# Turned x laid out by quarter, and the last batch's seven second-layer products in another order

## The chip, the cores and the metric

The kernel runs on one core of a Trainium2 chip. The metric is device time in microseconds (us) of one execution. Engines are named as the profile does: PE is TensorE's matmuls and PEld its weight loads, DVE is VectorE, ACT ScalarE, POOL GpSimd and SP the engine whose queue issues every DMA of this kernel. A name with a q behind it (SPq) is that engine's instruction queue.

## The reference

An attention with a local window and block sums, and behind it a mixer with two token layers and two channel layers:

```python
# q, k, v: (4, 8, 768, 64); block 32, window 16
k_sum, v_sum = k.reshape(B, H, 24, 32, D).max(3), v.reshape(B, H, 24, 32, D).mean(3)
scores_l = where(|i - j| < 16, scale * q @ k.T, -1e9)
scores_s = scale * q @ k_sum.T + log(32)
a = softmax(concat[scores_l, scores_s])            # with + 1e-9 in the sum
x = (a @ concat[v, v_sum]) -> (4, 768, 512)        # heads side by side
h  = relu(x.T @ w_tok1) @ w_tok2                   # 768 -> 256 -> 768 tokens
u  = x + h.T
h2 = relu(u @ w_ch1) @ w_ch2                       # 512 -> 1536 -> 512 channels
out = u + h2                                       # (4, 768, 512)
```

All in float32. The host lays inputs out and turns the result back; the kernel writes out as (batch, channel, token).

## The kernel before, in words

**Split operands.** A float32 product is made of three matmuls in the faster fp32r type: each operand is rounded (ACT, the "high" part), the rest is the difference (DVE or POOL, the "low" part), and high x high, high x low and low x high are summed in PSUM. The function `halved` makes such a pair.

**Stages.** Batches 0 to 2 go through attention, then token layers (`tok1*`, `tok2`), then the channel layers in 24 steps (two halves of tokens, twelve blocks of the 1536 channels): `ch1` (tile hp, result h) and `ch2` (tile acc). While batch b is in its channel layers, the attention of batch b + 1 runs between its steps. The last batch (b = 3) computes its channel layers in `last_batch` with seven products in place of eight (Winograd's form of Strassen's scheme): sums and differences of the four quarters of the weights ("mixed weights") and of u or h. POOL and ACT compute the mixed weights while batches 0 to 2 run (`mixes`, tiles wa and wc, which are stored to DRAM as mix_w1h, mix_w1l, mix_w2h, mix_w2l). `mixed_weight` loads one set back over a place in w1 or w2 that the products no longer need. Each set has a number, 0 to 3.

**Turning x.** For batches 2 and 3 (FAR = 2) the attention's result x, with tokens in the partitions, is turned so that channels are: DVE transposes each block of 32 x 32 (`turn_x`, L679, into tile xb), SP stores the tile to DRAM (L690, xaway), and SP fetches it in four parts of 32 partitions each (`fetch`, L571). In partition p of the DRAM tile stand the blocks of quarter q = p / 32, and part r of the fetch takes from each of the four quarters the blocks of r. Batch 2's land in tiles xT, batch 3's in the tiles uf (`sums_at`). `turn_blocks` turns the attention's weights e in the same way (tiles away and eT).

**Use of turned x.** In batch 2, `tok2` adds the token layers' result to xT (L922) and makes its two halves (L929 on ACT, L935 on DVE or POOL). In batch 3, `tok2_last` adds to uf (L1208), and `halved` makes the halves z (L1178, L1183); `turned` makes the differences of u (L1222).

**The last seven products.** They are named by their operand of h: "11", "21", "22", "4", "2", "3", "1" (before). Each is 36 matmuls in PSUM tiles pz, pz, pr, pv, pw, px, py (`sum_of`, L1232, two row blocks o = 0 and 1). `differ` makes differences of h (L1458), `operands` their halves (L1440, L1445 or `halved`); the halves stand in places that earlier weights or operands have left (`homes`). `into` and `summed` add a result to uf (L1256, L1509), `store` writes a finished row block (L1494).

**What sets the order.** Every instruction is given to a planner with an engine, a time that it is taken for, a rank, and what it reads and writes. The planner plays the run through with these times and writes each engine's instructions in the order that it finds; each engine then works through its queue in that order and waits in place. An issue on SP is played with 0.06 or 0.4 us on its queue, and a transfer with kb / 250 us of a common line and 2.2 us of landing. Slots of one tag are used in turn, with as many buffers as the tag has.

Of the kernel before, what the change touches and what calls it, by code (L numbers as in the profile page):

```python
# [199 lines left out]
def tile_attention_mixer(  # L200
# [343 lines left out]
    def turn_blocks(p, g):  # L544

        e = e_t[p, g]
        away = plan.slot(dram, [P, 2 * HS], F32, "away", f"away_{p}_{g}", 3)
        t_sb = sbuf([P, 2, HS], "e", f"eT_{p}_{g}", 3)
        for j in range(2):
            eT_t[2 * p + j, g] = (lambda j=j: t_sb.t[:, j]), [(t_sb, r) for r in range(P // 32)]  # L550
        add(
            "dve", 1.05, lambda: nc.vector.transpose(flat(e.t), flat(e.t)),
            reads=[(e, "ends")], writes=[(e, part) for part in PARTS], rank=R_ATT,
        )
        add(
            "sp", 0.4, lambda: nc.sync.dma_start(out=away.t, in_=flat(e.t)),
            reads=[(e, part) for part in PARTS], writes=[(away, 0)], kb=393,
        )

        state["turned"] = fetch(away, t_sb, lambda: flat(t_sb.t), 150)  # L560

    def flat(t):
        return t.rearrange("p j c -> p (j c)")

    def fetch(away, slot, view, kb, behind=()):


        def part(r):
            rows = slice(32 * r, 32 * (r + 1))
            src = away.t.rearrange("(q p) (t k) -> p t q k", p=32, k=P)  # L570
            nc.sync.dma_start(  # L571
                out=view()[rows].rearrange("p (t q c) -> p t q c", q=P // 32, c=32),
                in_=src[..., rows],
            )

        return [
            add(
                "sp", 0.4, lambda r=r: part(r), reads=[(away, 0)], writes=[(slot, r)], kb=kb,
                behind=behind,
            )  # L580
            for r in range(P // 32)
        ]
# [90 lines left out]
    def turn_x(b, p):  # L673

        x2, a = x_t[b, p]
        e = sbuf([P, S], "e", f"xb_{b}_{p}", 3)
        add(
            "dve", 1.05,
            lambda: nc.vector.transpose(  # L679
                e.t.rearrange("p (t c) -> p t c", c=P), x2.t[:, :, a, :]  # L680
            ),
            reads=x_keys(b, p), writes=[(e, 0)], rank=R_ATT,
        )
        for half, nt in enumerate(HT[b]):
# [4 lines left out]
            add(  # L689
                "sp", 0.4, lambda away=away, cs=cs: nc.sync.dma_start(out=away.t, in_=e.t[:, cs]),  # L690
                reads=[(e, 0)], writes=[(away, 0)], kb=nt // 2,
            )

    def fetch_x(b, half, p):
        if b == B - 1:
            slot = sums_at(half, p)
            return fetch(
                xa_t.pop((b, half, p)), slot, lambda: slot.t, HT[b][half] // 5, state["turned"]
            )
        tag, bufs = (("e", 3), ("ot", 2))[half]  # L700
        slot = xT_t[b, half, p] = sbuf([P, HT[b][half]], tag, f"xT_{b}_{half}_{p}", bufs)
        fetch(xa_t.pop((b, half, p)), slot, lambda: slot.t, HT[b][half] // 5)

    def spent(nt, quarter, half):

# [176 lines left out]
    def tok2(b, half, p):  # L882
# [34 lines left out]
        if far:  # L917
            xT = xT_t.pop((b, half, p))
            parts = [(xT, r) for r in range(P // 32)]
            add(  # L920
                "dve", spent(nt, 0.42, 0.6),
                lambda: nc.vector.tensor_tensor(  # L922
                    out=xT.t, in0=pt.t[:, :nt], in1=xT.t, op=ALU.add
                ),
                reads=[(pt, 0)], writes=parts, rank=R_EVAC,
            )
            add(
                "act", spent(nt, 0.38, 0.5),
                lambda: nc.scalar.activation(u.t[:, 0], xT.t, AF.Copy),  # L929
                reads=parts, writes=[(u, 0)], rank=R_EVAC,  # L930
            )
            eng, took = (("dve", spent(nt, 0.42, 0.62)), ("pool", spent(nt, 0.7, 1.2)))[half]
            add(
                eng, took,
                lambda: (nc.vector, nc.gpsimd)[half].tensor_tensor(  # L935
                    out=u.t[:, 1], in0=xT.t, in1=u.t[:, 0].bitcast(F32), op=ALU.subtract
                ),
                reads=[*parts, (u, 0)], writes=[(u, 1)], rank=R_EVAC,
            )
            return  # L940
# [248 lines left out]
    def tok2_last(half, p):  # L1189
        b, t1, u = B - 1, t1_t[B - 1, p], sums_at(half, p)  # L1190
        pt = bank(f"up_{b}_{half}_{p}", EIGHT if half else BANKS[1])

        def products():
            for k in range(DTOK // P):
                ks = slice(k * P, (k + 1) * P)
                for i, (w, part) in enumerate(((wt2h, 0), (wt2l, 0), (wt2h, 1))):
                    nc.tensor.matmul(  # L1197
                        pt.t[:, :HS], lhsT=t1.t[:, part, ks],
                        rhs=w.t[:, k, HS * half : HS * (half + 1)],
                        start=(k == 0 and i == 0), stop=(k == DTOK // P - 1 and i == 2),  # L1200
                    )

        add(
            "pe", 1.08, products, reads=t1_keys(b, p) + T2_KEYS, writes=[(pt, 0)], rank=R_ATT
        )
        add(
            "dve", 0.56,
            lambda: nc.vector.tensor_tensor(out=u.t, in0=pt.t[:, :HS], in1=u.t, op=ALU.add),  # L1208
            reads=[(pt, 0)], writes=rows4(u), rank=R_H,
        )  # L1210
# [51 lines left out]
    def last_batch():  # L1262
# [204 lines left out]
        for i in range(0, HF, 2):  # L1467
            differ(i, "11", "12", "11")
            differ(i, "12", "22", "12")
            differ(i, "22", "22", "11")  # L1470
            differ(i, "21", "21", "22")
        for n, of in (("4", "21"), ("2", "22"), ("3", "12"), ("1", "11")):
            operands(n, of, R_ATT)

        def sum_of(name, f0, c0, pts, begin, sets):
# [12 lines left out]
        def pair(name):  # L1488
            return [bank8(f"{name}{o}") for o in range(2)]

        def store(half, row, slot):
            add(
                "sp", 0.06,
                lambda: nc.sync.dma_start(  # L1494
                    out=out[b, row * P : (row + 1) * P, half * HS : (half + 1) * HS], in_=slot.t
                ),
                reads=rows4(slot), kb=196,
            )

        def us(half, row):  # L1500
            slot = sum_t[half, row]
            return slot, rows4(slot)

        def summed(half, row, x):

            slot, keys = us(half, row)
            add(
                "dve", 0.56,
                lambda: nc.vector.tensor_tensor(out=slot.t, in0=slot.t, in1=x.t, op=ALU.add),  # L1509
                reads=[(x, 0)], writes=keys, rank=R_EVAC,  # L1510
            )

        def into(pts, half, row, done=False):
            for o in range(2):
                out_of(pts[o], us(half, row + o), us(half, row + o))
                if done:
                    store(half, row + o, sum_t[half, row + o])
# [12 lines left out]
        into(v, 0, 2)  # L1530
        w = pair("pw")
        sum_of("2", 0, 0, w, True, None)
        for o in range(2):
            out_of(w[o], one(t[o]), one(t[o]))
            summed(1, o, t[o])
        x = pair("px")
        sum_of("3", HF, 0, x, True, None)
        for o in range(2):
            out_of(x[o], one(u3[o]), one(t[o]))
            summed(0, 2 + o, u3[o])  # L1540
            store(0, 2 + o, sum_t[0, 2 + o])
            summed(1, 2 + o, u3[o])
# [322 lines left out]
```

## Time and profile before

| | |
|---|---|
| Times of three runs | 567.02, 563.09, 565.91 us (median 565.91) |
| The profiled execution | 563.82 us, its span 562.0 us |
| PE busy | 547.2 us of the span |
| DVE, ACT, POOL busy | 333.0, 252.7, 246.6 us |
| Granted clock of TensorE, mean | 0.994 |
| DMA | 101.10 MB in 143279 packets |

The span is from the first to the last instruction of the profiled execution; the time is around it. In a row of instructions stand line, engine, operation, tile written, tiles read, shape, count, and in brackets how long the engine had stood idle before it and what it waited for. Rows that end in "x4" are several alike, told together. In rows of one source line the three numbers are the least, the median and the most of one instruction in ns.

### The profile page before, as it was taken

The page shows a single profiled execution, that of the slowest core. Times are in us where ns is not written, and L with a number is a line of the kernel's source. Part 1 is how long each engine was busy: PE and PEld are TensorE (multiplying, and loading weights), DVE is VectorE, ACT ScalarE, POOL GpSimd, SP SyncE. Part 2 cuts the span into 40 slices and gives each one's busy share as a digit, 9 for nine tenths or more (in the row PEclk, how much of TensorE's full clock was granted, in tenths as well). Part 3 has the DMA queues.
Part 4 walks back from the last instruction along what each step waited for, and adds up shares of the span by engine and source line. Part 5 has one row for each costly group of instructions (what it writes and reads, how often), then busy time and mean ns, then how long its engine had stood idle before and what let it go on. Part 6 is the DMA issues. An engine that isn't in the chain of part 4 may idle for free. (4 is left out here: it accounts for less than half of the span.)

```text
span 562.0 us, 12604 instructions
## 1 busy us (share of the span) xinstructions
PE 547.2 (97%) x4557; PEld 481.7 (86%) x4557; DVE 333.0 (59%) x922; ACT 252.7 (45%) x784; POOL 246.6 (44%) x362
## 2 busy tenths in 40 slices
PE   7889999999999999999999999999999998999997
PEld 4678888888999978888799987788889998999996
DVE  3788999979365355553553256344442047669973
ACT  4777675625585444322414334244333334356600
POOL 0316697834574932310068303468869753000000
PEclk9899999999999999999999999999999999999999
DMA  8953768755567147877685416888686545932732
GB/s 278 335 176 98 222 194 262 228 177 184 189 198 252 41 145 214 212 199 209 168 233 127 107 29 194 173 225 225 157 258 136 120 134 160 320 111 74 228 119 84
DMA packets 143279, 101.10 MB, mean 180 GB/s; under 512 B 88560, under 2 KB 123504, under 8 KB 143216
## 3 DMA queue, kind: packets, MB, share of 16 engines
q1 hardware_dynamic: 143216, 100.29, 61.7%
q8 instruction: 36, 0.59, 0.5%
q14 instruction: 27, 0.22, 0.1%
HBM read 70.18 MB, written 28.31 MB: 175 GB/s over the span
## 5 line engine op out<-in xcount | busy, mean ns | idle before, releaser
L1008 PE MATMUL acc<-h,w2h 128*128 128x256 f32 (+1 forms) x576 | 153.8, 339 | 0.0
L965 PE MATMUL hp<-u,w1h 128*128 128x256 f32 (+1 forms) x576 | 143.8, 339 | 0.0
L1008 PEld LDWEIGHTS acc<-h,w2h 128*128 128x128 f32 x576 | 100.6, 188 | 13.7 <-ACT h L977 1.6
L965 PEld LDWEIGHTS hp<-u,w1h 128*128 128x128 f32 x576 | 98.0, 189 | 12.4 <-issue 1.1
L491 ACT ACTIVATE e<-e,den 128x120 f32<-128x120 f32 x192 | 73.4, 384 | 52.5 <-DVE den L481 45.5
L965 PE MATMUL hp<-u,w1l 128*128 128x256 f32 (+1 forms) x288 | 96.9, 336 | 0.0
L1008 PE MATMUL acc<-h,w2l 128*128 128x256 f32 (+1 forms) x288 | 96.4, 335 | 0.0
L982 DVE SCALAR_TENSOR_TENSOR h<-hp,h 128x512 fp32r<-128x512 f32 (+1 forms) x72 | 39.9, 554 | 84.0 <-ACT h L977 83.8
L977 ACT ACTIVATE h<-hp 128x512 fp32r<-128x512 f32 (+1 forms) x72 | 35.1, 488 | 112.0 <-PE hp L965 111.2
L965 PEld LDWEIGHTS hp<-u,w1l 128*128 128x128 f32 x288 | 54.4, 189 | 5.8
L1008 PEld LDWEIGHTS acc<-h,w2l 128*128 128x128 f32 x288 | 54.2, 188 | 5.2
L481 DVE CUSTOM_DVE_ANT_0 e<-sc,mask_sb 128x120 f32<-128x120 f32 x192 | 41.7, 277 | 18.3 <-PE sc L467 16.8
L607 POOL TENSOR_SCALAR rec<-den 128x6 f32<-128x6 f32 x32 | 8.7, 272 | 66.9 <-ACT e L491 64.8
L491 ACT ACTIVATION_READ_ACCUMULATOR e<-e,den 128x1 f32 x192 | 36.1, 188 | 0.0
L1048 POOL TENSOR_TENSOR ot<-ot,u 128x512 f32<-128x512 f32 (+1 forms) x24 | 24.4, 1045 | 17.0 <-DVE ot L1040 15.4
L467 PE MATMUL sc<-k,q 64*64 64x120 f32 x768 | 29.5, 280 | 2.2 <-DVE den L481 2.0
L467 PEld LDWEIGHTS sc<-k,q 64*64 64x64 f32 x768 | 21.6, 138 | 11.2 <-issue 6.2
L906 PE MATMUL up<-wt2h,t 128*128 128x512 f32 (+1 forms) x96 | 28.4, 354 | 0.6 <-DVE t L725 0.6
L601 PEld LDWEIGHTS av<-v,eT 120*64 120x64 f32 x768 | 24.0, 138 | 4.9 <-issue 2.4
L601 PE MATMUL av<-v,eT 120*64 120x64 f32 x768 | 26.5, 224 | 1.0 <-DMA eT<-away 0.5
L335 DVE TENSOR_REDUCE ks<-k 128x24 f32<-128x768 f32 x16 | 15.2, 950 | 20.1 <-DMA k<-in_kw 20.1
L423 DVE TENSOR_REDUCE vs<-vb 96x8 f32<-96x256 f32 (+1 forms) x40 | 17.8, 459 | 13.0 <-DMA vb<-in_vb 12.8
(246 smaller groups left out, 1046.8 us busy)
## 6 DMA issues: line engine op xcount, KB each, us to landing
w<-in_w_ch SPq DMA_DIRECT2D x48, 256.0 KB
k<-in_kw SPq DMA_DIRECT2D x16, 720.0 KB
v<-in_vw SPq DMA_DIRECT2D x32, 288.0 KB
q<-in_q SPq DMA_DIRECT2D x16, 384.0 KB
away<-e SPq DMA_DIRECT2D x16, 384.0 KB
eT<-away SPq DMA_DIRECT2D x64, 96.0 KB
w<-in_w_tok SPq DMA_DIRECT2D x12, 256.0 KB
vb<-in_vb SPq DMA_DIRECT2D x32, 96.0 KB
```

The costliest lines, as they stand in the source:

```text
L335: lambda: nc.vector.tensor_reduce(out=ks.t.rearrange("p (t r) -> p t r", r=2), in_=kt.t[:, :, 16 : 16 + QT].rearrange("p t (r c) -> p t r ...
L423: lambda: nc.vector.tensor_reduce(out=s.t[:VB, rows], in_=slot.t[:VB], axis=AX, op=ALU.add),
L467: nc.tensor.matmul(tiles[j].t[c * QT : (c + 1) * QT, i * NC : (i + 1) * NC], lhsT=qt.t[rows, t * QT : (t + 1) * QT], rhs=kt.t[rows, t, :], ...
L481: nc.vector.tensor_tensor_reduce(out=e.t[:, j, i * P : i * P + NC], in0=tiles[j].t[:, i * NC : (i + 1) * NC], in1=mask_sb[:, mv, :], op0=A ...
L491: nc.scalar.activation(ei, ei, AF.Exp, bias=den_t[n].t[:, 1, T : T + 1], scale=-1.0, accum_out=den_t[n].t[:, 0, T : T + 1],)
L601: nc.tensor.matmul(pv[cs, T], lhsT=eT[:NC, T % (TT // 2), cs], rhs=v.t[:NC, 2 * T + c], start=True, stop=True,)
L906: nc.tensor.matmul(pt.t[:, :nt], lhsT=t1.t[:, part, ks], rhs=w.t[:, k, h0 : h0 + nt], start=(far and k == 0 and i == 0), stop=(k == DTOK / ...
L965: nc.tensor.matmul(pt.t[:, :nt], lhsT=block(w, f, c), rhs=us[c].t[:, part], start=(i == 0), stop=(i == len(ops) - 1),)
L977: lambda: nc.scalar.activation(h.t[:, 0], pt.t[:, :nt], AF.Relu),
L982: lambda: nc.vector.scalar_tensor_tensor(out=h.t[:, 1], in0=pt.t[:, :nt], scalar=0.0, in1=h.t[:, 0].bitcast(F32), op0=ALU.max, op1=ALU.sub ...
L1008: nc.tensor.matmul(slot.t[:, c0 : c0 + nt], lhsT=block(w, f, o), rhs=h.t[:, part], start=(f == 0 and w == "w2h" and part == 0 and o % n == 0),
L1048: lambda view=view, u=u: nc.gpsimd.tensor_tensor(out=view(), in0=view(), in1=u.t[:, 1].bitcast(F32), op=ALU.add),
```

## The change

Four things are changed.

1. `turn_x` writes its 32 x 32 blocks in the order (r, t, s) instead of (t, r, s): all blocks that part r will fetch stand side by side, for all six groups t of 128 tokens. One DMA stores the tile (before: one for each half of the tokens). `fetch_x` takes, from each of the four quarters q, one run: 384 bytes in batch 3, 512 and 256 bytes in batch 2 (before: runs of 128 bytes). The fetched tile's columns then stand in the order (q, t, s), quarter first.
2. What reads or adds to such a tile does so through permuted views (`from_sources`, `turned_to`, `turned_back`, `in_order`): in batch 2 the add and the two halves, after which u stands in the old order; in batch 3 the add of the token layers' result. The last batch's u stays in the new order through both channel layers, and the last add of each row block puts it back into the old order, into a tile of its own (tag t1), which is stored.
3. The last seven products run as "11", "21", "22", "2", "3", "1", "4". A21's differences and operand "4" come last. "3" is summed over the columns from c0 = 2 and "1" from c0 = 0, and three sets of mixed weights are loaded to other places: behind "11" set 2 (as before), behind "21" set 1, behind "22" set 0; none behind "4".
4. The planner is told of other sizes: 48 instead of 77 for a fetch of 48 KB, and one store of 393 instead of two.

```diff
-        state["turned"] = fetch(away, t_sb, lambda: flat(t_sb.t), 150)
+        state["turned"] = fetch(
+            away, t_sb,
+            lambda rows: away.t.rearrange("(q p) (t k) -> p t q k", p=32, k=P)[..., rows],
+            lambda t: flat(t).rearrange("p (t q c) -> p t q c", q=P // 32, c=32), 150,
+        )
...
-                e.t.rearrange("p (t c) -> p t c", c=P), x2.t[:, :, a, :]
+                e.t.rearrange("p (r t s) -> p t r s", r=P // 32, s=32),
+                x2.t[:, :, a, :].rearrange("p t (r s) -> p t r s", s=32),
...
-        for half, nt in enumerate(HT[b]):
-            cs = slice(H0[b][half], H0[b][half] + nt)
-            away = xa_t[b, half, p] = plan.slot(
-                dram, [P, nt], F32, f"xaway{nt}", f"xaway_{b}_{half}_{p}", 8
-            )
-            add(
-                "sp", 0.4, lambda away=away, cs=cs: nc.sync.dma_start(out=away.t, in_=e.t[:, cs]),
-                reads=[(e, 0)], writes=[(away, 0)], kb=nt // 2,
-            )
+        away = xa_t[b, p] = plan.slot(dram, [P, S], F32, "xaway", f"xaway_{b}_{p}", 8)
+        add(
+            "sp", 0.4, lambda: nc.sync.dma_start(out=away.t, in_=e.t),
+            reads=[(e, 0)], writes=[(away, 0)], kb=393,
+        )
...
+        fetch(
+            away, slot,
+            lambda rows: away.t.rearrange("(q p) (r t s) -> p r q t s", p=32, r=P // 32, s=32)[
+                :, rows.start // 32, :, ts
+            ],
+            from_sources, nt // 8, behind,
+        )
...
-                    out=xT.t, in0=pt.t[:, :nt], in1=xT.t, op=ALU.add
+                    out=from_sources(xT.t), in0=turned_back(pt.t[:, :nt]),
+                    in1=from_sources(xT.t), op=ALU.add,
...
-                lambda: nc.scalar.activation(u.t[:, 0], xT.t, AF.Copy),
+                lambda: nc.scalar.activation(in_order(u.t[:, 0]), turned_to(xT.t), AF.Copy),
...
-            lambda: nc.vector.tensor_tensor(out=u.t, in0=pt.t[:, :HS], in1=u.t, op=ALU.add),
+            lambda: nc.vector.tensor_tensor(
+                out=from_sources(u.t), in0=turned_back(pt.t[:, :HS]), in1=from_sources(u.t),
+                op=ALU.add,
+            ),
...
-            ("11", G0[:3]), ("21", [G0[3], *G1[:2]]), ("22", [*G1[2:], "x"]), ("4", ["v", "q", "x"]),
-            ("2", G0[:3]), ("3", [G0[3], *G1[:2]]), ("1", [*G1[2:], "x"]),
+            ("11", G0[:3]), ("21", [G0[3], *G1[:2]]), ("22", [*G1[2:], "x"]), ("2", ["v", "q", "x"]),
+            ("3", G0[:3]), ("1", [G0[3], *G1[:2]]), ("4", [*G1[2:], "x"]),
...
+            to = sbuf([P, HS], "t1", f"out_{half}_{row}", 4)
+            add(
+                "dve", 0.56,
+                lambda: nc.vector.tensor_tensor(
+                    out=turned_back(to.t), in0=from_sources(x()), in1=from_sources(slot.t),
+                    op=ALU.add,
+                ),
+                reads=[got, *keys], writes=[(to, 0)], rank=R_H,
+            )
...
-        sum_of("21", HF, 0, z, False, (0, HF, 0))
+        sum_of("21", HF, 0, z, False, (1, HF, 0))
...
-        sum_of("22", 0, 2, r, True, None)
+        sum_of("22", 0, 2, r, True, (0, 0, 1))
         into(r, 1, 0)
-        v = pair("pv")
-        sum_of("4", HF, 2, v, True, (1, HF, 1))
-        into(v, 0, 2)
...
-        sum_of("3", HF, 0, x, True, None)
+        sum_of("3", 0, 2, x, True, None)
...
-        sum_of("1", HF, 2, y, True, None)
+        sum_of("1", HF, 0, y, True, None)
         into(y, 1, 0, True)
         into(y, 1, 2, True)
+        v = pair("pv")
+        sum_of("4", HF, 2, v, True, None)
+        into(v, 0, 2, True)
```

More of the change, by code (lines that the diff above doesn't have):

```diff
@@ L558, in turn_blocks, with fetch @@
         )
-        state["turned"] = fetch(away, t_sb, lambda: flat(t_sb.t), 150)
+        state["turned"] = fetch(
[3 more added lines that the diff above has]
+        )
     def flat(t):
         return t.rearrange("p j c -> p (j c)")
[L565 to L573, printed above, removed]
-            )
+    def fetch(away, slot, src, view, kb, behind=()):
         return [
             add(
-                "sp", 0.4, lambda r=r: part(r), reads=[(away, 0)], writes=[(slot, r)], kb=kb,
-                behind=behind,
+                "sp", 0.4,
+                lambda r=r: nc.sync.dma_start(
+                    out=view(slot.t[32 * r : 32 * (r + 1)]), in_=src(slice(32 * r, 32 * (r + 1)))
+                ),
+                reads=[(away, 0)], writes=[(slot, r)], kb=kb, behind=behind,
             )
@@ L683, in turn_x, with from_sources, turned_to, turned_back @@
         )
-        for half, nt in enumerate(HT[b]):
-            cs = slice(H0[b][half], H0[b][half] + nt)
-            away = xa_t[b, half, p] = plan.slot(
-                dram, [P, nt], F32, f"xaway{nt}", f"xaway_{b}_{half}_{p}", 8
-            )
-            add(
-                "sp", 0.4, lambda away=away, cs=cs: nc.sync.dma_start(out=away.t, in_=e.t[:, cs]),
-                reads=[(e, 0)], writes=[(away, 0)], kb=nt // 2,
-            )
+        away = xa_t[b, p] = plan.slot(dram, [P, S], F32, "xaway", f"xaway_{b}_{p}", 8)
[3 more added lines that the diff above has]
+        )
     def fetch_x(b, half, p):
+        nt, away = HT[b][half], xa_t[b, p]
+        ts = slice(H0[b][half] // P, (H0[b][half] + nt) // P)
         if b == B - 1:
[L696 to L702, printed above, removed]
+            slot, behind = sums_at(half, p), state["turned"]
+        else:
+            tag, bufs = (("e", 3), ("ot", 2))[half]
+            slot = xT_t[b, half, p] = sbuf([P, nt], tag, f"xT_{b}_{half}_{p}", bufs)
+            behind = ()
+        fetch(
[5 more added lines that the diff above has]
+        )
+    def from_sources(t):
+        return t.rearrange("p (q t s) -> p q t s", q=P // 32, s=32)
+    def turned_to(t):
+        return from_sources(t).rearrange("p q t s -> p t q s")
+    def turned_back(t):
+        return in_order(t).rearrange("p t q s -> p q t s")
+    def in_order(t):
+        return t.rearrange("p (t q s) -> p t q s", q=P // 32, s=32)
     def spent(nt, quarter, half):
@@ L935, in tok2 @@
                 lambda: (nc.vector, nc.gpsimd)[half].tensor_tensor(
-                    out=u.t[:, 1], in0=xT.t, in1=u.t[:, 0].bitcast(F32), op=ALU.subtract
+                    out=in_order(u.t[:, 1]), in0=turned_to(xT.t),
+                    in1=in_order(u.t[:, 0]).bitcast(F32), op=ALU.subtract,
                 ),
@@ L1470, in last_batch @@
             differ(i, "22", "22", "11")
-            differ(i, "21", "21", "22")
-        for n, of in (("4", "21"), ("2", "22"), ("3", "12"), ("1", "11")):
+        for n, of in (("2", "22"), ("3", "12"), ("1", "11"), ("4", "21")):
+            if n == "1":
+                for i in range(0, HF, 2):
+                    differ(i, "21", "21", "22")
             operands(n, of, R_ATT)
@@ L1489, in pair, with us, summed @@
             return [bank8(f"{name}{o}") for o in range(2)]
-        def store(half, row, slot):
+        def us(half, row):
+            slot = sum_t[half, row]
+            return slot, rows4(slot)
+        def summed(half, row, x, got, done=False):
+            slot, keys = us(half, row)
+            if not done:
+                add(
+                    "dve", 0.56,
+                    lambda: nc.vector.tensor_tensor(
+                        out=slot.t, in0=x(), in1=slot.t, op=ALU.add
+                    ),
+                    reads=[got], writes=keys, rank=R_H,
+                )
+                return
+            to = sbuf([P, HS], "t1", f"out_{half}_{row}", 4)
+            add(
+                "dve", 0.56,
+                lambda: nc.vector.tensor_tensor(
+                    out=turned_back(to.t), in0=from_sources(x()), in1=from_sources(slot.t),
+                    op=ALU.add,
+                ),
+                reads=[got, *keys], writes=[(to, 0)], rank=R_H,
+            )
             add(
@@ L1494, in store @@
                 lambda: nc.sync.dma_start(
-                    out=out[b, row * P : (row + 1) * P, half * HS : (half + 1) * HS], in_=slot.t
+                    out=out[b, row * P : (row + 1) * P, half * HS : (half + 1) * HS], in_=to.t
                 ),
[L1497 to L1510, printed above, removed]
+                reads=[(to, 0)], kb=196,
             )
@@ L1514, in into, with added @@
             for o in range(2):
-                out_of(pts[o], us(half, row + o), us(half, row + o))
-                if done:
-                    store(half, row + o, sum_t[half, row + o])
+                summed(half, row + o, lambda o=o: pts[o].t[:, :HS], (pts[o], 0), done)
+        def added(half, row, slot, done=False):
+            summed(half, row, lambda: slot.t, (slot, 0), done)
         t, z = t_sum[4:], pair("pz")
@@ L1534, in last_batch @@
             out_of(w[o], one(t[o]), one(t[o]))
-            summed(1, o, t[o])
+            added(1, o, t[o])
         x = pair("px")
-        sum_of("3", HF, 0, x, True, None)
+        sum_of("3", 0, 2, x, True, None)
         for o in range(2):
             out_of(x[o], one(u3[o]), one(t[o]))
-            summed(0, 2 + o, u3[o])
-            store(0, 2 + o, sum_t[0, 2 + o])
-            summed(1, 2 + o, u3[o])
+            added(0, 2 + o, u3[o])
+            added(1, 2 + o, u3[o])
         y = pair("py")
-        sum_of("1", HF, 2, y, True, None)
+        sum_of("1", HF, 0, y, True, None)
         into(y, 1, 0, True)
         into(y, 1, 2, True)
+        v = pair("pv")
+        sum_of("4", HF, 2, v, True, None)
+        into(v, 0, 2, True)
     jobs = []
```

## The prediction

> **What bounds the kernel now.** I read the page first, then who waited for whom, then the stages, then the two places where TensorE stood still.
>
> ```profile
> span 562.0 us, 12604 instructions
> PE 547.2 (97%) x4557; PEld 481.7 (86%) x4557; DVE 333.0 (59%) x922; ACT 252.7 (45%) x784; POOL 246.6 (44%) x362
> ...
> DMA packets 143279, 101.10 MB, mean 180 GB/s; under 512 B 88560, under 2 KB 123504, under 8 KB 143216
> ```
>
> TensorE (PE) is busy 547.2 of 562.0 us: the whole idle time is 14.8 us. The change keeps the number and shape of the matmuls, so it can only take from, or add to, that idle time. The stages say where it lies (after a stage's length stand the busy time of PE, its weight loads, DVE, ACT and POOL, then PE's granted clock, the DMA engines' share and GB/s):
>
> ```profile
> 0.00:100.00 100.00, 91.90 (x967) 73.84 (x968) 81.42 (x231) 66.94 (x211) 51.52 (x82) 0.97 0.71 224
> 200.00:467.00 267.00, 265.21 (x2109) 227.73 (x2107) 119.69 (x382) 97.65 (x335) 129.03 (x203) 1.00 0.66 173
> 467.00:558.00 91.00, 90.41 (x522) 90.07 (x522) 67.19 (x106) 35.31 (x64) 4.34 (x5) 1.00 0.49 155
> 558.00:562.00 4.00, 0.00 (x0) 0.00 (x0) 1.02 (x2) 0.00 (x0) 0.00 (x0) 0.96 0.27 98
> ...
> 425.00:455.00 30.00, 30.00 (x251) 28.31 (x250) 7.18 (x18) 11.75 (x33) 22.96 (x30) 1.00 0.59 128
> ```
>
> The granted clock is 1.00 while PE works behind 200 us. Of the idle time 8.1 us lie in the first 100 us, before any instruction the change touches (the first is the turning of x for batch 2, after 225 us). Behind 200 us PE waits 1.79 + 0.59 us, and then comes a tail of 4.0 us. The waits behind 200 us are just two:
>
> ```profile
> PE up L1197 <- DVE h L982: 1.8, 1, 1.8
> PE av L601 <- DMA eT<-away: 0.5, 1, 0.5
> ```
>
> So the most that can be won is 1.85 + 0.5 us and a piece of the tail.
>
> **Where the 1.85 us come from.** The rows of the time line around it, with what each waited for in brackets:
>
> ```profile
> 430.96 6.65 SPq L571 DMA_DIRECT2D uf<-xaway  x10
> ...
> 445.72 1.01 SPq L690 DMA_DIRECT2D xaway<-xb  x2
> 446.78 3.58 SPq L571 DMA_DIRECT2D uf<-xaway  x4
> 450.46 0.55 SPq L1136 DMA_DIRECT2D mix_w2h<-wa_w_None  x1
> 451.06 3.46 SPq L571 DMA_DIRECT2D uf<-xaway  x5
> 454.61 0.56 SPq L1136 DMA_DIRECT2D mix_w2l<-wc_w_None  x1
> ```
> ```profile
> 442.54 1.31 POOL L1120 TENSOR_TENSOR wc_w_None<-wc_w_None,wa_w_None 128x512 fp32r<-128x512 f32 x1
> ...
> 453.66 2.54 POOL L1079 TENSOR_TENSOR wa_w_None<-w2h,w2l 128x512 f32<-128x512 f32 x2 [5.92 <-DMA mix_w2h<-wa_w_None]
> 457.71 1.43 POOL L1101 TENSOR_TENSOR wc_w_None<-wa_w_None 128x256 f32<-128x256 f32 x2 [1.51 <-DMA mix_w2l<-wc_w_None]
> ```
> ```profile
> 459.87 0.63 ACT L1113 ACTIVATE wa_w_None<-wc_w_None 128x512 fp32r<-128x512 f32 x1 [5.26 <-POOL wc_w_None L1101]
> ...
> 461.01 1.31 DVE L1183 TENSOR_TENSOR z<-uf,z 128x384 fp32r<-128x384 f32 x1 [4.20 <-ACT z L1178]
> ...
> 462.97 0.28 PE L965 MATMUL hp<-u,w1l 128*128 128x256 f32 x1
> ...
> 466.69 0.36 ACT L977 ACTIVATE h<-hp 128x256 fp32r<-128x256 f32 x1
> ...
> 467.56 0.44 PE L1197 MATMUL up<-wt2h,t 128*128 128x384 f32 x1 [1.85 <-DVE h L982]
> ```
>
> Read it backwards. PE waits for the last h; that h stands in ACT's queue behind the halves z of the new u; the z chain starts only at 459.87, because ACT stands 5.26 us at a rounding of mixed weights (L1113) that needs POOL; POOL had waited 5.92 and 1.51 us for its buffers, which are free when they have been stored; and the store of wc was issued at 454.61 although POOL had finished the tile at 443.85. It stood in SP's queue behind fetches of x. The rows of that queue follow each other without a pause until 455.17, and ten fetches take 6.65 us: 0.665 us each. **The queue of fetches of x is what ends last there**, and it is what the change makes shorter.
>
> **The change part by part.**
>
> *Fewer and longer runs.* A fetch today moves 48 KB (L571, last batch) in runs of 128 bytes, 384 of them; changed, 128 runs of 384 bytes, and one dimension less. Batch 2's go from 128 to 512 and 256 bytes. The number of fetches stays at 64; the stores of turned x fall from 16 to 8. What a fetch takes of SP's queue:
>
> ```profile
> L571 SPq DMA_DIRECT2D eT<-away x64: 557/658/3857, 215.3 to 424.4; - x64
> L571 SPq DMA_DIRECT2D xT<-xaway x32: 557/611/1393, 301.1 to 358.6; - x32
> L571 SPq DMA_DIRECT2D uf<-xaway x32: 563/628/2322, 425.2 to 453.9; - x32
> ```
>
> 768 runs (eT), 512 and 256 (xT) and 384 (uf) cost much the same, 0.56 us at the least, so the count of runs hardly sets the issue. Nearest are the stores of mixes between them, also of three dimensions: the one at 450.46 takes 0.55, and 0.60 passes until the next starts. Lower end: plain two-dimensional loads, of which the first and the last of twelve start 5.16 us apart, 0.47 each:
>
> ```profile
> 517.69 0.32 SPq L1149 DMA_DIRECT2D w2h<-mix_w2h  x1
> ...
> 522.85 0.38 SPq L1149 DMA_DIRECT2D w2l<-mix_w2l  x1
> ```
>
> I take 0.60, the row that is most like it. Of the 32 fetches 27 stand ahead of 450.46, and one of the two stores of x (1.01 us): 27 x 0.065 + 0.5 = 2.3 us earlier; the five fetches ahead of 454.61 make it 2.6. At 0.47 it would be 32 x 0.195 + 0.5 = 6.7; if only the store goes, 0.5. The delay passes 1:1 down the chain above, so 2.6 us against a wait of 1.85: the wait goes, **-1.85 us**; at the worst end 1.35 of it stay. What is late next is PE itself: hp is done at 463.25 and PE has other work until 465.71.
>
> [...] No row here has runs of 384 bytes.
>
> *The wait for eT* is on four fetches issued at 352.61, behind four of x in SP's queue:
>
> ```profile
> 347.10 2.70 SPq L571 DMA_DIRECT2D xT<-xaway  x4
> ...
> 352.61 2.76 SPq L571 DMA_DIRECT2D eT<-away  x4
> ```
>
> With 0.065 us off each of the four I take **-0.3 us**, between 0 and -0.5.
>
> *Permuted views.* The adds of x, the halves of batch 2 and the last adds read or write runs of 32 elements. Eight stream transposes write in another block order. Counts are the same. Rows:
>
> ```profile
> L612 DVE TENSOR_TENSOR x<-av,rec x32: 519/548/558, 19.9 to 431.4; 128x384 f32<-128x384 f32 x32
> L1208 DVE TENSOR_TENSOR uf<-up,uf x8: 544/546/558, 455.2 to 468.9; 128x384 f32<-128x384 f32 x8
> L335 DVE TENSOR_REDUCE ks<-k x16: 943/952/956, 5.0 to 373.8; 128x24 f32<-128x768 f32 x16
> ```
>
> L612 writes runs of 64 elements and costs what the plain L1208 costs; L335 reads runs of 32 and does 768 elements in 952 ns, 1.24 ns each, as do plain ops of 768 elements here. I take nothing. The far end is a doubling of L1208, 0.55 us each; a gain is excluded, as the element count stays. DVE, ACT and POOL have room in 323 to 372 us (batch 2: PE waits for none of it).
>
> *Order of the last products.* Each takes 6.26 us on PE, unchanged. Ready times of operands relax: today twelve differences of 0.96 us (the last is below) precede the operands that are due at 532.93; changed, nine do, so DVE is some 3 us earlier for that product, and A21's are due only in the end. But one set of weights gets closer: the one that is loaded as "22" ends is due in "3", with one product between; today at least two lie between ("2" and "3", before "1").
>
> ```profile
> 526.67 6.26 PE pr L1232 x36
> ```
> ```profile
> 524.61 1.44 SPq L1149 DMA_DIRECT2D w2h<-mix_w2h  x1
> ...
> 531.90 0.38 SPq L1494 DMA_DIRECT2D out<-uf  x1
> ```
> ```profile
> 528.25 0.96 DVE L1458 TENSOR_TENSOR h_h<-h_h,h_u 128x768 f32<-128x768 f32 x1
> ```
>
> Twelve loads at 0.47 us behind that store run from 532.3 to 537.9; with the 3.1 us that a store took to free its buffer (454.61 to 457.71) the last lands at 541.0. "3" starts at 539.2 and needs the last pair five sixths through its first half, at 541.8. It fits by 0.8 us: **0**. If the group stretches to the 7.3 us that the one before takes today (524.61 to 531.90), PE waits 0.9.
>
> *Tail.* Today the last product feeds two rows, and so two adds and two stores behind PE's end:
>
> ```profile
> 558.01 1.02 DVE L1256 TENSOR_TENSOR uf<-py,uf 128x384 f32<-128x384 f32 x2 [2.12 <-PE py L1232]
> ...
> 555.92 3.48 SPq L1494 DMA_DIRECT2D out<-uf  x3
> ```
>
> The issue of the last store ends at 559.40, and the span 2.6 us later. Changed, one add (0.56) and one store stand there: 1.02 - 0.56 = **-0.46 us**, at best -0.9 if the store also lands faster alone. The adds now write another tile (four buffers, eight rows); the buffers' former stores were issued 6 us earlier, so no wait.
>
> *Sum:* -1.85 - 0.3 - 0.46 = **-2.6 us**. The profiled execution took 563.82 us around its span of 562.0, so it would take 561.2. The three runs' median, 565.91, is 2.1 above that; the four executions together average 564.96, and from that I predict **562.4 us**.
>
> **Rivals.**
>
> *It does nothing for the wait, and the tail alone remains* (25%). A planner writes all queues from due times, and from batch 2 on it sees other ones (48 instead of 77 for a fetch). The h may be queued as late again, behind more z. For it: only the order put four z ahead of the h. Against it: the lateness starts in SP's queue. Time: 564.96 - 0.5 = 564.5.
>
> *The queues' order turns against PE, slower* (20%). Place: DVE and ACT between 455 and 468 us. The planner counts 0.4 us for a fetch that takes 0.60 or more, and can now put all eight pairs of add and z ahead of the last h instead of four. An add and its z (0.55 each, L1208 above) take 1.1 us of the chain, so four more make the wait 1.85 + 4.4 - 2.6 = 3.65, 1.8 longer; with tail and eT off, +1.0: 566.0. With only 0.5 us won in SP's queue it is +3.1. The same chain is where dear views would show: at 0.55 us more on four adds the wait is 1.85 - 2.6 + 2.2 = 1.45, and the tail loses its gain. It decides from 3.4 us of further delay on (1.85 + 0.76 + the 0.75 that the wait has to spare). [...]
>
> *The weights of "3" come late* (10%): +0.9 us as above, -1.7 in all: 563.3.
>
> The forecast has the remaining 45%.
>
> **Range and chances.** Low end: all bounds together, -1.85 - 0.5 - 0.9 = -3.25, on the fastest run (563.09): 559.8. High end: the slower rival's +3.1 on the average gives 568.1, and its +1.0 on the median 566.9; I set 567.8. The four executions lie 0.7% apart, so 1% is about what can be told from no change. Faster by 1% would need 560.2, which is below what the waits hold (5.7 us against at most 3.3): 6%, for runs that fall well. Slower by 1% would need three such waits in new places: 7%. Within 1%: 87%.
>
> **What would show it.** Right: no PE wait on h near 466 us; fetches of x at 0.60 us or less from start to start; the store of wc issued 2 us earlier; one add behind PE's end; of 88,560 packets under 512 bytes 18,432 fewer (24,576 of 128 bytes become 4,096 of 384 and 2,048 of 256). Wrong: a PE wait of over 1 us behind 225 us, between 455 and 468 us or in px's first half above all; L1208 or L922 much over their time of before; SP still late at 450 us.

## The result, and the profile after

| | before | after |
|---|---|---|
| Median (18 runs each) | 564.48 us | 560.88 us |
| Lowest to highest | 562.16 to 567.02 | 559.55 to 563.75 |
| The profiled execution, its span | 563.82, 562.0 | 559.61, 557.8 |

The ratio after / before is 0.9942, with a 95% interval from 0.9926 to 0.9959: 3.3 us less, between 2.3 and 4.2. The prediction was 562.4 us, in a range from 559.8 to 567.8.

The head of the page after:

```profile
span 557.8 us, 12595 instructions
PE 544.0 (98%) x4557; PEld 479.6 (86%) x4557; DVE 330.3 (59%) x922; ACT 251.9 (45%) x784; POOL 246.8 (44%) x362
...
DMA packets 125743, 101.10 MB, mean 181 GB/s; under 512 B 70000, under 2 KB 105456, under 8 KB 125680
```

The matmuls are the same 4557, and 18,560 fewer packets are under 512 bytes (18,432 were counted on). By the idle time of PE: the view of its waits has no row behind 200 us now, where before had two (1.8 us on the last h, 0.5 on eT). The stages of the changed kernel say it too (columns as in the prediction; the first is a stage's bounds, the second its length, the third PE's busy time):

```profile
0.00:20.00 20.00, 15.44 (x263) 9.52 (x267) 10.89 (x58) 11.86 (x51) 2.06 (x10) 1.00 0.92 304
...
200.00:463.00 263.00, 263.00 (x2094) 225.96 (x2093) 118.84 (x384) 97.31 (x334) 129.89 (x203) 1.00 0.64 174
463.00:553.40 90.40, 90.40 (x528) 90.38 (x527) 66.97 (x106) 34.92 (x63) 3.46 (x4) 1.00 0.50 158
```

263.00 of 263.00 and 90.40 of 90.40: from 200 us to the last product PE doesn't stop. Against before:

- **Waits behind 200 us**: 2.35 us to 0.
- **Tail**, from PE's end to the end of the span: 4.0 us (557.99 to 562.0) to 3.5 (554.28 to 557.8).
- **The first 20 us**, which the change doesn't touch. The same stage of before:

```profile
0.00:20.00 20.00, 17.09 (x213) 10.58 (x214) 9.20 (x56) 10.98 (x46) 2.04 (x10) 0.83 0.92 308
```

The granted clock was 0.83 there and is 1.00 after. PE did 263 matmuls in 15.44 us where it had done 213 in 17.09, and the first turning of x in batch 2 starts 1.3 us earlier, though nothing of the code ahead of it differs. So of the 4.2 us between the two spans about 1.3 belong to this pair of executions and not to the change; 2.85 are left. The medians differ by 3.6, and 2.85 lies in the interval. The last 0.7 us I can't put to a row.

**Where the 1.85 us went.** The SP queue of the changed kernel (start and length in us, then the instructions told together):

```profile
427.06 5.14 SPq L574 DMA_DIRECT2D uf<-xaway  x10
...
438.30 1.52 SPq L685 DMA_DIRECT2D xaway<-xb  x1
439.87 5.25 SPq L574 DMA_DIRECT2D uf<-xaway  x8
...
445.55 0.34 SPq L1152 DMA_DIRECT2D mix_w2h<-wa_w_None  x1
445.94 0.43 SPq L574 DMA_DIRECT2D uf<-xaway  x1
446.48 0.71 SPq L1152 DMA_DIRECT2D mix_w2l<-wc_w_None  x1
```

Ten fetches take 5.14 us in place of 6.65, 0.51 each in place of 0.665. From the first fetch of the last batch to the store of wc it is now 23.1 us, and was 29.4 (425.19 to 454.61): 6.3 us less. Of them about five are the 32 fetches (32 x 0.155). The rest is a balance of pauses: before's queue had one in three fetches, 3.68 us where three take 2.0 (the row below), and one in the four from 446.78; the changed kernel's has one in the eight from 439.87, 5.25 us where eight take 4.1, and its one store of x takes 1.52 us where the two of before took 1.01.

```profile
426.57 3.68 SPq L571 DMA_DIRECT2D uf<-xaway  x3
```

Then down the chain of the changed kernel, on POOL, ACT and PE:

```profile
448.49 2.54 POOL L1095 TENSOR_TENSOR wa_w_None<-w2h,w2l 128x512 f32<-128x512 f32 x2 [2.35 <-DMA mix_w2h<-wa_w_None]
...
453.27 0.63 ACT L1129 ACTIVATE wa_w_None<-wc_w_None 128x512 fp32r<-128x512 f32 x1 [0.27 <-POOL wc_w_None L1117]
...
461.75 0.39 ACT L993 ACTIVATE h<-hp 128x256 fp32r<-128x256 f32 x1 [1.49 <-PE hp L981]
...
463.95 0.34 PE L1213 MATMUL up<-wt2h,t 128*128 128x384 f32 x1
```

The brackets are what to read. POOL waits 2.35 us for the stores in place of 5.92 and 1.51. ACT stands 0.27 us at the rounding (L1129) in place of 5.26. ACT now waits 1.49 us for hp ahead of the last h: it has caught up with PE, and h no longer stands behind late work. The row of PE has no bracket: it waits for nothing.

### The profile page after: what moved, and what is told of

It reads as the page before. It is cut to its first block, busy times and chain, and to the rows that moved or that the text cites. A ratio compares the mean times of both kernels' runs of the same rounds, so it can differ in the third digit from the quotient of the medians.

```text
span 557.8 us, 12595 instructions
## 1 busy us (share of the span) xinstructions
PE 544.0 (98%) x4557; PEld 479.6 (86%) x4557; DVE 330.3 (59%) x922; ACT 251.9 (45%) x784; POOL 246.8 (44%) x362
## 4 chain that ended last, share of the span: by engine, by line
PE 90%; ACT 4%; DVE 3%; POOL 2%; issue 1%; ACTq 0%
PE acc L1024 27%; PE hp L981 27%; PE sc L467 4%; PE av L599 4%; PE up L920 3%; PE t1q L837 3%; ACT e L491 2%; PE x L1251 2%; PE y L1251 2%; PE z L1251 2%; PE pz L1251 2%; PE t1q L800 2%; PE up L1213 2%; PE warm L1731 1%; PE pw L1251 1%; PE pv L1251 1%
## 5 line engine op out<-in xcount | busy, mean ns | idle before, releaser
L467 PE MATMUL sc<-k,q 64*64 64x120 f32 x768 | 28.0, 271 | 3.7 <-DVE den L481 2.2
```

The lines of the kernel that those rows point to most:

```text
L467: nc.tensor.matmul(tiles[j].t[c * QT : (c + 1) * QT, i * NC : (i + 1) * NC], lhsT=qt.t[rows, t * QT : (t + 1) * QT], rhs=kt.t[rows, t, :], ...
```

## The experiments

The product order and the layout can be separated, so two kernels split the change.

**The products alone** (`order_only`): the kernel before, with the lists of the last batch changed (line numbers are this kernel's own).

```diff
-  ("11", G0[:3]), ("21", [G0[3], *G1[:2]]), ("22", [*G1[2:], "x"]), ("4", ["v", "q", "x"]),
-  ("2", G0[:3]), ("3", [G0[3], *G1[:2]]), ("1", [*G1[2:], "x"]),
+  ("11", G0[:3]), ("21", [G0[3], *G1[:2]]), ("22", [*G1[2:], "x"]), ("2", ["v", "q", "x"]),
+  ("3", G0[:3]), ("1", [G0[3], *G1[:2]]), ("4", [*G1[2:], "x"]),
...  (and the order of differ, operands and sum_of, the sets of weights in other places)
```

> The kernel before, with the new order of the last seven products and the new places of the weights alone; x is turned, stored and fetched as before. If the late fetches of x are the cause of the waits: the tail alone is won, -0.5 us (ratio 0.999), and PE still waits 1.85 us for the last h near 467 us and 0.5 us for eT. If the order of the products and the planning that follows from it carry the gain: -2 to -3.6 us, and no wait on h.

Measured: 0.9991 [0.9971, 1.0011], the ratio to the kernel before with its 95% interval, as in all runs below. PE's two waits, and the last add:

```profile
357.02 1.27 PE L601 MATMUL av<-v,eT 120*64 120x64 f32 x36 [0.99 <-DMA eT<-away]
```
```profile
PE up L1197 <- DVE h L982: 0.9, 1, 0.9
```
```profile
556.38 0.56 DVE L1256 TENSOR_TENSOR uf<-pv,uf 128x384 f32<-128x384 f32 x1 [2.58 <-PE pv L1232]
```

Both waits are still there, 0.99 us for eT at 357 us and 0.9 on the last h, 1.9 in sum where before has 2.35. (A further 0.35 us for eT stands at 223.87, ahead of the first turning of x.) The wait on h is 0.9 shorter because SP's pause is: the three fetches that took 3.68 us take 2.48 in this execution. Behind PE's end stands one add, and the tail is 3.5 us. The order brings about half a us, at the end, and no more.

**The layout alone** (`layout_only`): the changed kernel with the old lists and the old order of products.

> The changed kernel with the products in the old order and the old places of weights; only the layout of turned x, its one store and its longer runs are new. If the late fetches are the cause: -2.3 us (ratio 0.996), no wait of PE behind 225 us, two adds and two stores behind PE's end as before. If the order carries the gain: -0.5 us or less, and a wait on h of about 1.8 us.

Measured: 0.9964 [0.9945, 0.9983]. The only wait of PE behind 200 us, and what DVE does behind PE's end:

```profile
226.90 1.27 PE L599 MATMUL av<-v,eT 120*64 120x64 f32 x36 [0.48 <-DMA eT<-away]
```
```profile
557.05 1.49 DVE L1529 TENSOR_TENSOR out<-py,uf 128x384 f32<-128x384 f32 x3 [2.58 <-PE py L1251]
```

The wait on h is gone with the layout, and with it alone. So is the wait on eT near 357 us: the one in the row above stands at 226.90, ahead of this kernel's first turning of x (228.89), where no fetch of x has been issued yet. The order of ACT's work is that of before, all six halves z ahead of the last h. In this mixture the planner left three adds to the end, so the tail is 4.5 us, 0.5 worse than before. The two parts give 0.09% and 0.36%, and 0.45% in sum, against 0.58% [0.41, 0.74] for the whole: they add up.

**Is it the late store, or something else that the layout does?** (`stores_first`): the kernel before, its transfers unchanged; only the planner is told a longer issue and a better rank for the stores of mixes.

```diff
-                "sp", 0.4, lambda r=r: part(r), reads=[(away, 0)], writes=[(slot, r)], kb=kb,
+                "sp", 0.67, lambda r=r: part(r), reads=[(away, 0)], writes=[(slot, r)], kb=kb,
...
-                kb=2 * n,
+                kb=2 * n, rank=-1,
```

> The kernel before, with x turned and fetched as before; only the planner is told that a fetch takes 0.67 us of SP's queue (instead of 0.4) and that stores of mixed weights go ahead of it. In the list it writes, 13 of the 32 fetches of the last batch's x stand behind the store of wc for which POOL waits, instead of none. If the late store is the cause of the 1.85 us: POOL and ACT do not wait, no wait of PE on the last h, about -1.8 us (ratio 0.997) with the fetches as slow as before. If it is the landing of x itself that is late: the wait stays or grows, ratio 1.000 or above.

Measured: 0.9961 [0.9936, 0.9986], as much as the layout alone. SP's queue, the POOL instruction that had waited 5.92 us, and PE's only wait behind 200 us:

```profile
448.82 0.55 SPq L1136 DMA_DIRECT2D mix_w2l<-wc_w_None  x1
449.41 8.84 SPq L571 DMA_DIRECT2D uf<-xaway  x13
```
```profile
448.13 2.54 POOL L1079 TENSOR_TENSOR wa_w_None<-w2h,w2l 128x512 f32<-128x512 f32 x2
```
```profile
PE up L906 <- DVE den L481: 0.6, 1, 0.6
```

Thirteen fetches at 0.68 us now stand behind the store, POOL doesn't wait for it, and the wait on h is gone with runs of 128 bytes. But the new numbers moved something else too. On ACT the last h now stands ahead of all six halves z, where the kernel before and the changed one have it behind them:

```profile
459.00 0.38 ACT L977 ACTIVATE h<-hp 128x256 fp32r<-128x256 f32 x1 [0.38 <-PE hp L965]
...
462.00 0.53 ACT L1178 ACTIVATE z<-uf 128x384 fp32r<-128x384 f32 x1 [1.14 <-DVE uf L1208]
```

So this run shows that the wait can be planned away with the old transfers. It does not show which did it, the early store or the early h. That the late store is the cause rests on the changed kernel, `layout_only` and `double_issue`, in which h stays behind the six z.

**Both together** (`after_stores_first`): the changed kernel with the same rank for the stores, and 0.67 us told for its fetches of eT and 0.52 for those of x. Here too h moves ahead of the z.

> The changed kernel, with the planner told that stores of mixed weights go first and that a fetch takes 0.67 us (eT) or 0.52 us (x) of SP's queue. The changed kernel has no wait of PE left behind 225 us, so if those waits are the whole of what could be won there, nothing more comes: ratio 0.994 as the changed kernel, and new waits can only make it slower. If the shorter backlog of SP's queue has a worth of its own: ratio 0.991 or below.

Measured: 0.9941 [0.9919, 0.9962], no wait of PE behind 200 us. It equals the change: the waits were all that was to be won in this place.

**The issue made dearer** (`double_issue`): the changed kernel, each fetch of x given as two DMAs of 16 partitions.

```diff
+        def pieces(r):
+            n = 16 if view is from_sources else 32
+            for k in range(0, 32, n):
+                nc.sync.dma_start(
+                    out=view(slot.t[32 * r + k : 32 * r + k + n]),
+                    in_=src(slice(32 * r, 32 * (r + 1)))[k : k + n],
+                )
```

> The changed kernel, but each fetch of turned x is issued as two DMAs of 16 partitions: the same runs and bytes, twice the issues in SP's queue (the planner counts them as one). If SP's queue is what is late: 27 to 32 issues of 0.5 us more stand ahead of the store of the mixed weights, the store slips by 13 to 16 us, and the wait of PE on the last h comes back with 5 to 9 us: +5 to +9 us against the changed kernel (ratio to before 1.003 to 1.010). If it is the DMA engines' work on short runs that was late: no wait, ratio 0.994 as the changed kernel.

Measured: 1.0272 [1.0240, 1.0304], 579.71 us, 18.8 more than the changed kernel. The waits, SP's queue and ACT's rounding:

```profile
PE up L1218 <- DVE h L1003: 11.2, 1, 11.2
PE av L604 <- DMA eT<-away: 3.5, 2, 2.3
```
```profile
436.20 10.34 SPq L574 DMA_DIRECT2D uf<-xaway  x20
...
468.30 0.41 SPq L1157 DMA_DIRECT2D mix_w2l<-wc_w_None  x1
```
```profile
474.10 0.63 ACT L1134 ACTIVATE wa_w_None<-wc_w_None 128x512 fp32r<-128x512 f32 x1 [14.71 <-POOL wc_w_None L1122]
```

Half the bytes cost the same issue (20 in 10.34 us, 0.52 each), so what is paid is the issue and not the transfer. The same wait on the same h comes back through the same chain, and the wait on eT with it. The size was missed by a factor of two. I hadn't counted batch 2's doubled fetches: the last batch's first fetch starts 6.4 us later, and only 1.0 of that stood ahead of batch 2's first turning of x already. And these stalls cost more than their length. Stages in and behind the two stalls:

```profile
359.00:360.00 1.00, 0.00 (x0) 0.00 (x0) 0.00 (x0) 0.00 (x0) 0.00 (x0) 0.50 1.05 315
364.00:365.00 1.00, 1.00 (x3) 0.78 (x3) 0.02 (x1) 0.00 (x0) 0.00 (x0) 0.50 0.73 249
475.00:477.00 2.00, 0.00 (x0) 0.00 (x0) 1.75 (x3) 1.08 (x3) 1.94 (x2) 0.50 0.06 20
484.50:485.00 0.50, 0.50 (x5) 0.50 (x5) 0.11 (x1) 0.00 (x0) 0.00 (x0) 0.71 0.00 0
485.00:485.50 0.50, 0.50 (x7) 0.50 (x6) 0.28 (x1) 0.00 (x0) 0.00 (x0) 1.00 0.00 0
```

While PE stands for the h, the granted clock falls to 0.50. PE starts again at 481.73, and the clock is back before 485. Until the first product of `last_batch` PE then takes 3.94 us, where the changed kernel takes 2.47 for the same 18 matmuls: 1.5 us more. The waits on eT (1.24 and 2.25 us, with 0.57 us of matmuls between them) do the same: the clock falls to 0.50 and is back between 365 and 366 us. From those matmuls to the next `up` PE takes 6.9 us without the second wait, and 4.4 in the changed kernel: 2.5 us more. The waits (14.7 us) and the slow clock behind them (4.0) make up 18.7 of the 18.8 us.

The two places differ. In the stall on h the clock falls some 4 us after PE's last matmul (that one ends at 470.51, and from 470 to 475 the clock is 0.96 at the mean) and is back 3 us after the next, from 481.73 to within 484.50 to 485.00. The waits on eT are 1.24 and 2.25 us, both shorter than those 4 us, and the clock is back only after 5 us of work. Why they differ no run shows.

**The planner's sizes alone** (`sizes_only`), for the slower rival: the kernel before, its transfers unchanged, but the planner is told the changed kernel's smaller size of a fetch.

```diff
-                xa_t.pop((b, half, p)), slot, lambda: slot.t, HT[b][half] // 5, state["turned"]
+                xa_t.pop((b, half, p)), slot, lambda: slot.t, HT[b][half] // 8, state["turned"]
-        fetch(xa_t.pop((b, half, p)), slot, lambda: slot.t, HT[b][half] // 5)
+        fetch(xa_t.pop((b, half, p)), slot, lambda: slot.t, HT[b][half] // 8)
```

> The kernel before, but the planner is told of the changed kernel's sizes for fetches of x (48 instead of 77 for 48 KB); the transfers are those of before. In the list it writes, all 32 fetches stand ahead of both stores of the last w2 mix, as in the changed kernel nearly. If the planning carries the gain: no wait on h, ratio 0.996. If SP's queue is the cause: the store of wa slips by five fetches, 3.3 us, POOL starts some 1.8 us later than before, and the wait on h grows from 1.85 to about 3.6 us: ratio 1.003.

Measured: 1.0159 [1.0120, 1.0197], 573.55 us. PE's long wait, SP's queue and POOL's work:

```profile
PE t1q L823 <- POOL xs L867: 9.2, 1, 9.2
```
```profile
448.67 6.89 SPq L571 DMA_DIRECT2D uf<-xaway  x9
455.66 0.56 SPq L1136 DMA_DIRECT2D mix_w2h<-wa_w_None  x1
```
```profile
458.70 1.26 POOL L1079 TENSOR_TENSOR wa_w_None<-w2h,w2l 128x512 f32<-128x512 f32 x1 [12.19 <-DMA mix_w2h<-wa_w_None]
459.92 2.78 POOL L867 TENSOR_TENSOR xs<-x,xs 128x256 fp32r<-128x256 f32 x4
```

Told that fetches are small, the planner put more of them ahead of the stores, and on POOL it put the token layers' halves (xs) behind the next mix. The mix waits 12.19 us for its buffer, xs waits behind it in POOL's queue, and PE waits 9.2 us for xs. So the new sizes turn the order against PE unless the issues get shorter with them. It came five times dearer than expected and on another engine.

**What makes the issue of a fetch cheap?** Four kernels are the changed one with groups of 14 or 16 loads behind all outputs, which lengthens the time and changes nothing ahead. Each line below is one group on SP; its length over its count is close to the time from one start to the next.

`forms`, 48 KB a load: 32 runs of 1536 bytes; 128 of 384 from four quarters (the changed fetch); 384 of 128 in one row evenly; 384 of 128 in the order of the old fetch; 256 of 192.

> The changed kernel, and behind its last instructions five groups of sixteen loads of 48 KB into 32 partitions each, issued one behind the other with nothing else running: 32 runs of 1536 bytes; 128 of 384 (as the changed kernel fetches x); 384 of 128 evenly spaced; 384 of 128 in the order of the kernel before; 256 of 192. The time is longer by the groups and says nothing; the distance from start to start of the issues is read. If the number of dimensions sets the issue, as the prediction has it: 0.47 us for the first group and 0.60 for the other four alike. If the count of runs sets it: 0.47, 0.51, 0.66, 0.66, and 0.57 to 0.63 for the last.

```profile
557.66 7.34 SPq L1607 DMA_DIRECT2D form<-in_q  x16
...
568.30 8.07 SPq L1607 DMA_DIRECT2D form<-in_q  x16
...
579.62 11.15 SPq L1607 DMA_DIRECT2D form<-in_q  x16
...
594.17 11.25 SPq L1607 DMA_DIRECT2D form<-in_q  x16
```

0.46, 0.50, 0.70, 0.70 us (the fifth group took 0.70 too). The new form is cheap by itself, and 0.60 is in none of them. Two more kernels looked for the cause in the number and in the length of runs:

> The changed kernel, and behind its last instructions five groups of sixteen loads into 32 partitions each, issued one behind the other: 128 runs of 128 bytes, 192 of 128, 256 of 128, 384 of 128, 768 of 64. The distance from start to start is read. If the count of runs sets an issue with a step between 128 and 256 (0.50 and 0.70 us in the groups before): 0.50, then 0.60 to 0.70, then 0.70 three times. If the length of a run sets it (192 bytes and below are dear): 0.70 in all five. If it grows with the count: 0.50, 0.55, 0.60, 0.70, 0.95.

> The changed kernel, and behind its last instructions five groups of sixteen loads into 32 partitions each: 128 runs of 192 bytes, 128 of 256, 128 of 384, 192 of 256, 96 of 512. The distance from start to start is read. The groups before gave 0.64 us for 128 runs of 128 bytes and 0.50 for 128 of 384. If the length of a run sets the issue: 0.64, then 0.50 or less for the other four. If it is something else than the length in the two groups of before (a source whose runs lie far apart): 0.64 in all five.

In `forms2` 128, 192, 256, 384 and 768 runs took 0.64, 0.64, 0.65, 0.66 and 0.70 us. In `forms3` runs of 192, 256 and 384 bytes took 0.64 alike, 192 runs 0.64, and 96 runs of 512 bytes 0.66. Its third group has 128 runs of 384 bytes, just as the changed fetch, but 192 elements apart:

```profile
582.24 10.21 SPq L1599 DMA_DIRECT2D form<-in_q  x16
```

0.64 here against 0.50 above: neither count nor length. (384 runs out of one row stand in `forms` with 0.70 and in `forms2` with 0.66, so between two kernels such a time can differ by 0.04.) That leaves where a partition's runs lie (`forms4`, groups (a) to (e)):

> Five groups of 16 loads each, behind the kernel's outputs, so the time is longer by some 60 us. All groups but two move 128 runs; in three of them the four runs of a partition come from rows 32 apart (the quarters of a matrix), as in the changed kernel's fetches of x: (a) four far runs of 384 bytes, (b) four runs of 384 bytes 192 elements apart in one row, (c) four far runs of 128 bytes, (d) four far runs of 256 bytes, (e) two far runs of 768 bytes, 64 rows apart (64 runs in all). Theory that far-apart quarters make the issue cheap: (a), (c), (d) 0.50 us each start to start, (e) 0.46 to 0.50, (b) 0.64. Theory that it is something else in the earlier run (the neighbours of its group, the clearing before it): (a) and (b) alike, at 0.50 or at 0.64.

```profile
556.35 7.51 SPq L1603 DMA_DIRECT2D form<-in_q  x16
...
566.80 10.27 SPq L1603 DMA_DIRECT2D form<-in_q  x16
...
580.09 7.72 SPq L1603 DMA_DIRECT2D form<-in_q  x16
590.51 7.73 SPq L1603 DMA_DIRECT2D form<-in_q  x16
600.83 7.89 SPq L1603 DMA_DIRECT2D form<-in_q  x16
```

(a) 0.47, (b) 0.64, (c) 0.48, (d) 0.48, (e) 0.49 us. Two or four runs from rows 32 or 64 apart take 0.47 to 0.49, whether of 128 or 768 bytes; four runs out of one row take 0.64. Why far runs issue faster no run shows. Nor is far enough by itself: the old order in `forms` also reads four far quarters, with three runs near each other in each, and takes 0.70.

## Why the prediction was right, and where it was not

**PE's wait on h (-1.85):** right, by the chain that was named. `layout_only` removes it with the layout, and `double_issue` brings it back with the issue alone; in both ACT has the z and the last h in the order of before.

**The size of the issue (0.60 us):** wrong. "I take 0.60, the row that is most like it": the stores of mixes were not like it. The fetch took 0.51, near the lower end (0.47), so the 32 fetches gave some 5 us where 2.1 were counted. The choice rested on the number of dimensions, and the four forms kernels show three-dimensional loads from 0.47 to 0.70. The other 0.5 of the 2.6, for the store of x that falls away, did not come: the one store takes 1.52 us where two took 1.01 (0.38 in `layout_only`). Nor did the queue run "without a pause": the four fetches from 446.78 take 3.58 us, 0.9 each. All this cost the forecast nothing, since the wait held only 1.85 us.

**The transfers:** the prediction had no row with runs of 384 bytes. The 30 us from the first fetch on, after and then before (the last two columns are the DMA engines' share and GB/s):

```profile
423.40:453.40 30.00, 30.00 (x251) 28.32 (x250) 7.16 (x19) 11.86 (x34) 26.18 (x33) 1.00 0.54 145
```
```profile
425.20:455.20 30.00, 30.00 (x251) 28.31 (x251) 7.24 (x18) 11.75 (x33) 22.96 (x30) 1.00 0.59 126
```

The engines move 145 GB/s with 0.54 of their time, and moved 126 with 0.59: 20% less time for a byte, over all transfers of the stretch. By single packets, one of 128 bytes takes 13 ns at the mean in the stretch of before; in that of the changed kernel one of 384 takes 27 and one of 512 takes 28. So tripling a run gained: 27 ns in place of three times 13. In the sum it changed nothing, for `double_issue` shows the issue to be the limit: the same runs with twice the issues at 0.52 us each brought the wait on h back.

**The wait on eT (-0.3):** right in its place and cause, and all of the 0.5 us went. Near 357 us it stands in `order_only` (0.99 us) with the old fetches of x, in neither the changed kernel nor `layout_only` with the new ones, and in `double_issue` again (1.24 and 2.25 us) with twice the issues. The four fetches of x ahead of it take 1.85 us in place of 2.70, 0.85 less where 0.26 were counted. (`stores_first`, with another order in the queue, has no such wait either.)

**Permuted views (0):** right. The adds that read PSUM in runs of 32 elements, before 546 ns at the median:

```profile
L1224 DVE TENSOR_TENSOR uf<-up,uf x8: 545/558/558, 453.6 to 465.2; 128x384 f32<-128x384 f32 x8
```

12 ns, and not a doubling. The last adds, which also write so, take 552 to 558 ns at the median. In batch 2 the adds take 554 ns (550 before) and the halves on ACT 524 (526).

**Weights of "3" (0):** right. The last of the twelve loads is issued at 534.61, and "3" (px) runs its 6.26 us from 535.51 without a pause:

```profile
534.61 0.61 SPq L1165 DMA_DIRECT2D w2l<-mix_w2l  x1
```
```profile
535.51 6.26 PE px L1251 x36
```

**The tail (-0.46):** right. One add, 0.56 us in place of 1.02, and the tail 0.5 shorter:

```profile
554.31 0.56 DVE L1531 TENSOR_TENSOR out<-pv,uf 128x384 f32<-128x384 f32 x1 [2.58 <-PE pv L1251]
```

**The slower rival (20%):** it did not come, but its mechanism, a planner that counts too little for a fetch, is real: `sizes_only` has the new sizes without the shorter issues, and PE stands 9.2 us, on POOL's xs and not on the last h. Its price was worked out from a wrong reading. It lets four more pairs of add and z come ahead of the last h, but there are only six z, and ACT's rows of before have all six ahead of it (460.40 to 466.26). At most two adds could still come, so neither the 4.4 us nor the +1.0 and +3.1 made of it were there to be lost by this way.

**The sum:** 2.6 us counted, 2.8 found in rows (2.35 + 0.45), 3.3 in the ratio. The forecast of 562.4 is 1.5 us above the median: 0.5 because the base of four executions (564.96) lay above that of 18 (564.48), 0.2 from eT; the other 0.8, which lies within the measurement, I can't put to a row.

## What to carry to other kernels

When an engine stands at a buffer that is "waiting for its store", look at where the store stands in the issuing queue: here a tile that had been ready for over ten us waited behind fetches, thirteen of which could as well stand behind its store (`stores_first`). Telling the planner so, which also moved h, gave as much as rebuilding the transfers. What can be won is the wait, not what is saved on the queue: 6.3 us saved there gave 1.85. When a planner is told one new number, compare the order on every engine before naming the cause: the h that moved in `stores_first` is not in the edit. A time or size that a planner is told is part of the kernel: changed without the transfer that it describes, it cost 9 us on an engine that the change did not touch.

## What the hardware showed that was not expected

- In the forms kernels the time of an issue on SP went by how a load's runs lie: 0.47 us for four far runs to a partition (`forms4`, a), 0.64 for the same runs from one row (b), 0.70 for the old fetch's order (`forms`); bytes between 16 and 48 KB did not matter (0.47 to 0.48, a, c and d).
- The start of the same code differs between executions. The changed kernel and the four that only add loads behind its outputs start the first turning of x at 225.7 and 226.2 us with a granted clock of 1.00 in the first 20 us, at 226.6 and 227.7 with 0.91, and at 228.4 with 0.83. In these five a lower clock goes with a later start, but two executions at the same 0.91 differ by 1.1 us. All this is up to 2.7 us, nearly what the change is worth: align two traces at the first instruction of the same code before comparing spans.
- A stall of 11.2 us on PE was followed by 3 us at half the clock, 1.5 us more. Two stalls of 1.24 and 2.25 us close together were followed by 5 us at half the clock, 2.5 us more; a single one of 1.85 us in the kernel before was followed by none.
- A DMA packet of 384 bytes took nearly as long as one of 512 (27 and 28 ns at the mean, in the changed kernel from 423.4 to 453.4 us), and one of 128 took 13 (in the kernel before from 425.2 to 455.2).
